# Sliding-window attention and a routed MoE: q and k by head on a partition, turned by 64-column products

## Chip, cores and metric

One core of a Trainium2 chip. The metric is the device time of one execution in microseconds (us); lower is better. The kernel before takes 766.49 us (median of three runs, 764.59 to 767.16). The profiled execution has a span of 762.4 us from its first to its last instruction; the views below count from that span's start.

## What is computed

Eight batches with eight heads each of 576 positions with head size 64 go through causal attention with a window of 64. The result, 4608 rows of 512, goes through a layer with eight experts, in which every row goes to the one expert with the highest gate value. All data are float32.

```python
scores = scale * np.matmul(q, k.transpose(0, 1, 3, 2))
rel = pos[:, None] - pos[None, :]
mask = (rel >= 0) & (rel < 64)
attn = softmax(np.where(mask, scores, -1e9))
x = np.matmul(attn, v)                  # (8, 8, 576, 64), then (4608, 512)
logits = x @ w_gate                     # 8 experts
idx, gate = argmax(logits), softmax(logits)[idx]
out = gate * (np.maximum(x @ w1[idx], 0) @ w2[idx])   # w1: 512 x 1024, w2: 1024 x 512
```

## The kernel before

The attention works on 16 units: a pair of batches (`bg`) by a pair of heads (`g`). A unit has 9 tiles of 128 query positions, and is worked off in three steps of three tiles, so 48 steps. The first 512 positions of each batch (`SM`) are loaded with four consecutive positions on one partition (`NV` = 4); the last 64 of each, the "rests", are loaded for all heads at once. The scores need q and k turned, so that the head dimension lies on the partitions: the 64 of the first head on partitions 0 to 63, those of the second on 64 to 127.

Loads of q and k for a unit, one DMA for each batch, tensor and head. On a partition, the two heads of a position lie side by side, 64 values each:

```python
def load_qk(u):
    bg, g = units[u]
    qks[u] = [qk_m(((u % 3 + 2) % 3 * 2 + n) * 1024, BG, NV, 2, D) for n in range(2)]
    for i in range(BG):
        for t, src in zip(qks[u], (q, k)):
            for h in range(2):
                nc.sync.dma_start(                                     # L487
                    out=t[:, i, :, h, :],
                    in_=src[bg * BG + i, 2 * g + h, 0:SM, :].rearrange("(p j) d -> p j d", j=NV),
                )
```

Turning them, for a step: `c` is 0 or 1 for a batch's main part, 2 for the rests. A transpose takes 128 partitions by 128 values (two heads of one position) and writes every fourth column of a PSUM bank; ScalarE copies the bank out.

```python
def turned(s):
    u, c = divmod(s, NST)
    ...
    if c == BG:
        ...                                        # rests: two full transposes, L531
        return
    for n, t in enumerate(qks[u]):
        tr = banks[next(tr_ring)](0, NV, P)
        for j in range(NV):
            nc.tensor.transpose(                                       # L539
                out=tr.rearrange("d a b -> d (a b)").rearrange("d (p j) -> d j p", j=NV)[:, j, :],
                in_=t[:, c, j].rearrange("p h d -> p (h d)"), identity=ident[:]
            )
        to = Ts[u][:, n, c * NV : (c + 1) * NV, :].rearrange("d t s -> d (t s)")
        nc.scalar.copy(out=to, in_=tr.rearrange("d a b -> d (a b)"))   # L544
```

The order in which the engines get their work is that of the program. Before the loop and in each step:

```python
load_qk(0)
nc.sync.dma_start(out=wg[:, :, 0:E], in_=...)
nc.sync.dma_start(out=x_dram[NT : NT + 1, :], in_=zrow[:])
load_rests(0)              # 4 DMAs of q and k, 2 of v, all by SyncE
load_v(0)                  # 4 DMAs of v by SyncE; 6 copies by GpSimd (L511 to L517)
load_qk(1)
load_v(1)
load_qk(2)
...
def step(s):
    if 0 <= s + 1 < N:
        prs[s + 1] = softened(*masked(s + 1, scored(s + 1)))   # L572 scores, 64x64 blocks
    if 0 <= s - 1 < N:
        px = weighted(s - 1, pTs.pop(s - 1))                   # L618, 128x64 blocks
    ripe = 0 <= s - 3 < N and logit(s - 3)                     # L655, 128x32 blocks
    if 0 <= s < N:
        pTs[s] = flipped(prs.pop(s))                           # L603, 128x128 transposes
    ...                                                        # divided(s - 1), loads of unit u + 3
    if s + 3 < N:
        turned(s + 3)                                          # L539 or L531
    if 0 <= s - 2 < N:
        x_turned(s - 2)                                        # L643, 128x128 transposes
    ...
for s in range(-3, N):
    step(s)
```

`masked` runs on VectorE (L585), `softened` on ScalarE (L595). The second half of the kernel, the experts, is left as it is.

Of the kernel before, what the change touches and what calls it, by code (L numbers as in the profile page):

```python
# [12 lines left out]
BF16 = mybir.dt.bfloat16  # L13
I32 = mybir.dt.int32
AF = mybir.ActivationFunctionType
ALU = mybir.AluOpType
# [4 lines left out]
WINDOW = 64  # L21
MASKED = -1e9
# [14 lines left out]
def kernel(  # L37
# [10 lines left out]
    nc = tc.nc  # L48
    P = nc.NUM_PARTITIONS
    B, H, S, D = q.shape  # L50
# [8 lines left out]
    NV = NB // 2  # L59
    SM = NV * P  # L60
    BG = 2
# [15 lines left out]
    consts = ctx.enter_context(tc.tile_pool(name="consts", bufs=1))  # L77
# [4 lines left out]

    ident = consts.tile([P, P], F32, name="ident")
    make_identity(nc, ident[:])
    GE = 32
    wg = consts.tile([P, NG, GE], F32, name="wg")
    nc.gpsimd.memset(wg[:], 0.0)
# [12 lines left out]
    V, G = nc.vector, nc.gpsimd  # L100
# [76 lines left out]
    with tc.tile_pool(name="tmp", bufs=1) as tmp:  # L177
# [8 lines left out]
        for i in range(BG):  # L186
            iota(tok_g[:, :, i * NV : (i + 1) * NV], pattern=[[BG * S, NJ // NTB], [P, NV]], base=i * S,
                 channel_multiplier=1)
            iota(tok_g[i * D : (i + 1) * D, :, BG * NV], pattern=[[BG * S, NJ // NTB]], base=i * S + SM,
                 channel_multiplier=1)  # L190
# [8 lines left out]
            out=before[:], in_=ones[:], pattern=[[1, P]], compare_op=ALU.is_gt, fill=0.0, base=0,  # L199
# [34 lines left out]


    VW = D + 1
    ST = 3
    NST = NTB // ST
    UT = NTB * P
    qk_m = Memory(consts.tile([P, 10240], F32, name="qk_m"))  # L240
# [199 lines left out]
    with tc.manual_schedule(), ExitStack() as held, ExitStack() as brief:  # L440
# [3 lines left out]
        att = brief.enter_context(tc.tile_pool(name="att", bufs=2))  # L444
        xp = brief.enter_context(tc.tile_pool(name="xp", bufs=3))
        sc_ring, tr_ring = cycle((0, 1)), cycle((2, 3, 4, 5))


        NM = 2 + ST
        mask = consts.tile([P, NM, P], BF16, name="mask")  # L450
        nc.gpsimd.memset(mask[:], 0.0)
        for h in range(2):
            for m0, m1, first in ((0, 1, False), (1, 2, h == 0), (2, NM, False)):
                rows = slice(h * D, (h + 1) * D)
                sel = partial(
                    nc.gpsimd.affine_select, out=mask[rows, m0:m1, :], in_=mask[rows, m0:m1, :], fill=MASKED,
                )
                if first:
                    sel(pattern=[[0, m1 - m0], [-1, P]], compare_op=ALU.is_ge, base=0, channel_multiplier=1)
                else:  # L460
                    sel(pattern=[[0, m1 - m0], [1, P]], compare_op=ALU.is_gt, base=0, channel_multiplier=-1)
                    sel(pattern=[[0, m1 - m0], [-1, P]], compare_op=ALU.is_ge, base=WINDOW, channel_multiplier=1)
        NVR = 3
        v_ring = []
        for i in range(NVR):
# [12 lines left out]

        def load_qk(u):
            bg, g = units[u]
            qks[u] = [qk_m(((u % 3 + 2) % 3 * 2 + n) * 1024, BG, NV, 2, D) for n in range(2)]
            for i in range(BG):
                for t, src in zip(qks[u], (q, k)):
                    for h in range(2):
                        nc.sync.dma_start(  # L487
                            out=t[:, i, :, h, :],
                            in_=src[bg * BG + i, 2 * g + h, 0:SM, :].rearrange("(p j) d -> p j d", j=NV),
                        )  # L490

        def load_rests(bg):

            at = 6144 + bg % 2 * 2048
            vr = qk_m(at + 1024, BG, H, D)
            rests[bg] = [qk_m(at, H, D), qk_m(at + 512, H, D), vr]
            for t, src in zip(rests[bg], (q, k)):
                for i in range(BG):
                    nc.sync.dma_start(
                        out=t[i * D : (i + 1) * D], in_=src[bg * BG + i, :, SM:S, :].rearrange("h p d -> p h d")  # L500
                    )
            for i in range(BG):
                nc.sync.dma_start(out=vr[D:P, i], in_=v[bg * BG + i, :, SM:S, :].rearrange("h p d -> p h d"))

        def load_v(u):
            bg, g = units[u]
            va, vb = v_ring[u % NVR]
            for i in range(BG):
                for h in range(2):
                    nc.sync.dma_start(out=va[:, i, :, h, 0:D], in_=whole(v, u, i, h))  # L510
                G.tensor_copy(out=vb[D:P, i, NV - 1, :, 0:D], in_=rests[bg][2][D:P, i, 2 * g : 2 * g + 2])  # L511

                nc.gpsimd.tensor_copy(  # L513
                    out=vb[0:D, i].rearrange("p j h d -> p (j h d)"),
                    in_=va[D:P, i].rearrange("p j h d -> p (j h d)"),
                )
                nc.gpsimd.tensor_copy(  # L517
                    out=vb[D:P, i, 0 : NV - 1].rearrange("p j h d -> p (j h d)"),
                    in_=va[0:D, i, 1:NV].rearrange("p j h d -> p (j h d)"),
# [6 lines that stand above are left out]
            if c == 0:  # L526
                Ts[u] = qkT_m(u % 2 * 2 * NTB * P, 2, NTB, P)
            if c == BG:
                tr = banks[next(tr_ring)](0, NV, P)
                for n, t in enumerate(rests[bg][0:2]):  # L530
                    nc.tensor.transpose(  # L531
                        out=tr[:, n, :], in_=t[:, 2 * g : 2 * g + 2].rearrange("p h d -> p (h d)"), identity=ident[:]
                    )
                nc.scalar.copy(out=Ts[u][:, :, BG * NV, :], in_=tr[:, 0:2, :])
                return
            for n, t in enumerate(qks[u]):
                tr = banks[next(tr_ring)](0, NV, P)
                for j in range(NV):
                    nc.tensor.transpose(  # L539
                        out=tr.rearrange("d a b -> d (a b)").rearrange("d (p j) -> d j p", j=NV)[:, j, :],  # L540
                        in_=t[:, c, j].rearrange("p h d -> p (h d)"), identity=ident[:]
                    )
                to = Ts[u][:, n, c * NV : (c + 1) * NV, :].rearrange("d t s -> d (t s)")
                nc.scalar.copy(out=to, in_=tr.rearrange("d a b -> d (a b)"))  # L544

# [32 lines left out]
        def masked(s, scs):  # L578

            m0 = (1, 0, 2)[s % NST]  # L580
            prs = [att.tile([P, ST, P], F32, name=f"pr{h}") for h in range(2)]
            mx = small.tile([P, 2, ST], F32, name="mx")
            for h in range(2):
                for m in range(ST):
                    V.tensor_tensor_reduce(  # L585
                        out=prs[h][:, m, :], in0=scs[h][:, m, :], in1=mask[:, m0 + m, :], scale=-scale, scalar=-2 * MASKED,
                        op0=ALU.add, op1=ALU.min, accum_out=mx[:, h, m : m + 1],
                    )
            return prs, mx

        def softened(prs, mx):
            for h in range(2):
                for m in range(ST):
                    y = prs[h][:, m, :]
                    nc.scalar.activation(out=y, in_=y, func=AF.Exp, scale=-1.0, bias=mx[:, h, m : m + 1])  # L595
            return prs
# [276 lines left out]
            gather_first(perm_e[:, 0:C])  # L873

        N = NU * NST
        load_qk(0)
        nc.sync.dma_start(out=wg[:, :, 0:E], in_=moe_w_gate.rearrange("(g p) e -> p g e", p=P))
        nc.sync.dma_start(out=x_dram[NT : NT + 1, :], in_=zrow[:])
        load_rests(0)
        load_v(0)  # L880
        load_qk(1)
        load_v(1)
        load_qk(2)

        for g in range(NG):
            step = NST * (g // 2) + g % 2 + 1
# [7 lines left out]

        prs, pTs = {}, {}
        def step(s):
            if 0 <= s + 1 < N:
                prs[s + 1] = softened(*masked(s + 1, scored(s + 1)))
            if 0 <= s - 1 < N:
                px = weighted(s - 1, pTs.pop(s - 1))  # L900
            ripe = 0 <= s - 3 < N and logit(s - 3)
            if 0 <= s < N:
                pTs[s] = flipped(prs.pop(s))
            if 0 <= s - 1 < N:
                divided(s - 1, px)
            if s >= 0 and s % NST == 0:
                u = s // NST
                if u + 3 < NU and (u + 3) % NG == 0:
                    load_rests((u + 3) // NG)
                if u + 2 < NU:  # L910
                    load_v(u + 2)
                if u + 3 < NU:
                    load_qk(u + 3)
            if s + 3 < N:
                turned(s + 3)
            if 0 <= s - 2 < N:
                x_turned(s - 2)
            for op in todo.pop(s, ()):
                op()
            if ripe:  # L920
                bg, c = (s - 3) // (NG * NST), (s - 3) % NST
                parts = by_tokens(bg, c)
                next(parts)
                todo.setdefault(s + 1, []).append(partial(next, parts, None))
                if c == NST - 1:
                    after(s + 1, choose(bg), bg)


        for n, s in enumerate((N - 6, N - 3)):
            fs = slice(n * HF, (n + 1) * HF)  # L930
            todo.setdefault(s, []).append(partial(nc.sync.dma_start, out=w2s[0][:, fs], in_=w2v[0][:, fs]))
        for s in range(-3, N):
            step(s)
        assert not todo
        sums_w2(0)
# [135 lines left out]
```

## Time and profile before

| what | value |
|---|---|
| time, median of 3 | 766.49 us |
| span of the profiled execution | 762.4 us, mean granted TensorE clock 0.986 |
| attention stage, until the last step's weighted sums | 0 to about 199 us |
| TensorE busy, 0 to 10 and 10 to 20 us | 4.46 and 5.33 us |
| TensorE busy, 40 to 60 and 100 to 120 us | 19.86 and 20.00 us |
| DMA share, 0 to 10 and 10 to 20 us | 0.57 and 1.07 |
| DMA share, 40 to 60 and 100 to 120 us | 0.87 and 0.86 |
| moved over the span | 94.55 MB in 137,620 packets, 117,072 of them under 512 B |

A line of the timeline gives the start in us, the time until the last of the merged instructions has ended, the engine, the kernel's line, the operation with its output and inputs, for TensorE the rows and columns of the stationary block (128*64: 128 rows, 64 columns), the shape and the count; in brackets, how long the engine had been idle before, and what ended that. "SPq" is SyncE's queue: its lines are issues of DMAs, not the transfers. A line of the table of waits gives who waited for whom, the total in us, how often, and the longest.

### The profile page before, as it was taken

How to read it: one execution, taken by the hardware profiler on the slowest of the kernel's cores; microseconds unless marked ns; L12 is line 12 of the kernel's file. 1: busy time of each engine (PE TensorE's matmuls, PEld its weight loads, DVE VectorE, ACT ScalarE, POOL GpSimd, SP SyncE). 2: the span in 40 equal slices, each digit the busy share in tenths (PEclk: the TensorE clock that was granted, in tenths of full speed). 3: DMA queues.
4: the chain of work that ended last, by engine and by line, in shares of the span. 5: the costliest groups of instructions: out<-in, count | busy, mean ns of one | idle time of the engine just before them, and what ended most of it. 6: DMA issues, size and time to landing. Idle time of an engine off the chain costs nothing. (4 is left out here: it accounts for less than half of the span.)

```text
span 762.4 us, 18401 instructions
## 1 busy us (share of the span) xinstructions
PE 720.1 (94%) x7018; PEld 650.5 (85%) x7018; DVE 395.0 (52%) x1355; ACT 268.4 (35%) x676; POOL 357.1 (47%) x366
## 2 busy tenths in 40 slices
PE   4999999999899999999999999999999999999995
PEld 3888888887688988998999899899988899988994
DVE  2677997988758544523542353352434452424432
ACT  4888888887543201211121122011220121211220
POOL 5215558593860635537531653663266465262111
PEclk8999999999899999999999999999999999999998
DMA  8997889983513712604410360542171171101101
GB/s 162 226 205 173 175 181 255 213 225 113 195 42 126 277 58 67 229 29 138 159 56 30 96 208 30 166 142 70 31 257 45 40 254 56 43 24 42 43 29 54
DMA packets 137620, 94.55 MB, mean 124 GB/s; under 512 B 117072, under 2 KB 117072, under 8 KB 137490
## 3 DMA queue, kind: packets, MB, share of 16 engines
q1 hardware_dynamic: 127858, 62.16, 29.8%
q0 software_dynamic: 9056, 28.58, 11.7%
q10 hardware_dynamic: 576, 2.10, 0.8%
q8 instruction: 78, 1.28, 0.7%
q14 instruction: 52, 0.43, 0.2%
HBM read 73.94 MB, written 20.45 MB: 124 GB/s over the span
## 5 line engine op out<-in xcount | busy, mean ns | idle before, releaser
L322 PE MATMUL bank<-qk_m,s 128*128 128x128 f32 x1216 | 145.4, 275 | 0.0
L322 PEld LDWEIGHTS bank<-qk_m,s 128*128 128x128 f32 x1216 | 140.4, 192 | 0.0
L322 PE MATMUL bank<-qk_m,w 128*128 128x128 f32 x912 | 112.2, 276 | 12.5 <-DVE v_m L358 8.8
L272 POOL DMA_INDIRECT qk_m<-x_dram,at_g x42 | 44.6, 1063 | 167.5 <-PE bank L303 160.2
L322 PEld LDWEIGHTS bank<-qk_m,w 128*128 128x128 f32 x912 | 106.7, 192 | 17.5 <-issue 17.3
L595 ACT ACTIVATE pr<-pr,mx 128x128 f32<-128x128 f32 x288 | 89.7, 390 | 31.8 <-DVE mx L585 31.5
L358 DVE TENSOR_TENSOR v_m<-bank,v_m 128x256 f32<-128x256 f32 x101 | 40.8, 422 | 110.1 <-PE bank L362 54.8
L585 DVE CUSTOM_DVE_ANT_0 pr<-bank,mask 128x128 f32<-128x128 f32 x288 | 64.4, 286 | 27.7 <-PE bank L572 26.1
L329 ACT COPY qk_m<-bank 128x512 f32<-128x512 f32 x19 | 11.2, 587 | 165.7 <-PE bank L322 155.2
L292 POOL DMA_INDIRECT out_dram<-v_m,at_s x42 | 42.4, 1010 | 56.5 <-DVE v_m L358 44.7
L139 POOL TENSOR_TENSOR s<-w 128x1024 f32<-128x1024 f32 x22 | 52.3, 2376 | 19.1 <-DMA qk_m<-x_dram,at_g 14.8
L362 PE MATMUL bank<-qkT_m,v_m 128*128 128x256 f32 x240 | 54.0, 380 | 1.7 <-DVE v_m L139 1.7
L362 PEld LDWEIGHTS bank<-qkT_m,v_m 128*128 128x128 f32 x240 | 45.4, 190 | 8.5 <-DVE v_m L139 2.5
L362 PE MATMUL bank<-qk_m 128*128 128x256 f32 x224 | 52.1, 380 | 0.0
L513 POOL COPY v_m<-v_m 64x520 f32<-64x520 f32 x32 | 19.8, 618 | 67.0 <-DMA v_m<-in_v_dram 59.7
L618 PEld LDWEIGHTS bank<-v_m,pT 128*64 128x64 f32 x1152 | 40.5, 139 | 11.6 <-DVE xs L632 5.8
L618 PE MATMUL bank<-v_m,pT 128*64 128x65 f32 x1152 | 47.2, 229 | 2.6 <-DVE xs L632 2.6
L362 PE MATMUL bank<-s,v_m 128*128 128x256 f32 x216 | 48.1, 379 | 0.0
L362 PEld LDWEIGHTS bank<-qk_m 128*128 128x128 f32 x224 | 41.5, 190 | 5.5 <-ACT v_m L374 0.4
L362 PEld LDWEIGHTS bank<-s,v_m 128*128 128x128 f32 x216 | 41.0, 190 | 5.6
L572 PE MATMUL bank<-qkT_m 64*64 64x128 f32 x1152 | 44.8, 286 | 0.1
L539 PE MATMUL bank<-ident,qk_m 128*128 128x128 f32 x256 | 36.6, 287 | 8.7 <-DMA qk_m<-in_q_dram 8.1
(167 smaller groups left out, 1220.7 us busy)
## 6 DMA issues: line engine op xcount, KB each, us to landing
w<-in_moe_w_dram SPq DMA_DIRECT2D x11, 2048.0 KB, 9.2
qk_m<-in_q_dram SPq DMA_DIRECT2D x72, 128.0 KB, 3.8
qk_m<-in_k_dram SPq DMA_DIRECT2D x72, 128.0 KB, 3.7
v_m<-in_v_dram SPq DMA_DIRECT2D x64, 128.0 KB, 3.7
qk_m<-in_moe_w_dram SPq DMA_DIRECT2D x3, 2048.0 KB, 16.1
x_dram<-xs POOLq DMA_DIRECT2D x6, 512.0 KB, 4.8
x_dram<-xs POOLq DMA_DIRECT2D x3, 768.0 KB, 5.3
w<-in_moe_w_dram ACTq DMA_DIRECT2D x4, 512.0 KB, 5.0
```

Of the source, the lines that this page charges most:

```text
L139: op()
L272: G.indirect_dma_start(out=xg[c], out_offset=None, in_=x_dram[:, :], in_offset=bass.IndirectOffsetOnAxis(ap=at_g[:, c : c + 1], axis=0),)
L292: put = G.indirect_dma_start(out=out[:, :], out_offset=bass.IndirectOffsetOnAxis(ap=at_s[:, c : c + 1], axis=0), in_=ys[c], in_offset=None ...
L322: nc.tensor.matmul(acc[:, f, :], lhsT=a[:, g, f * P : (f + 1) * P], rhs=b[:, g, :], start=(first and f == 0 and g == 0), stop=(g == HG - 1 ...
L358: plus = lambda out, a, b: V.tensor_tensor(out=out, in0=a, in1=b, op=ALU.add)
L362: nc.tensor.matmul(acc, lhsT=a[:, f, :], rhs=b[:, f, :], start=(start and f == 0), stop=(stop and f == HF - 1), skip_group_check=True,)
L513: nc.gpsimd.tensor_copy(out=vb[0:D, i].rearrange("p j h d -> p (j h d)"), in_=va[D:P, i].rearrange("p j h d -> p (j h d)"),)
L539: nc.tensor.transpose(out=tr.rearrange("d a b -> d (a b)").rearrange("d (p j) -> d j p", j=NV)[:, j, :], in_=t[:, c, j].rearrange("p h d - ...
L572: nc.tensor.matmul(out_, lhsT=qT[rows, t, a * WINDOW : (a + 1) * WINDOW], rhs=rhs, start=True, stop=True, skip_group_check=True,)
L585: V.tensor_tensor_reduce(out=prs[h][:, m, :], in0=scs[h][:, m, :], in1=mask[:, m0 + m, :], scale=-scale, scalar=-2 * MASKED, op0=ALU.add, ...
L595: nc.scalar.activation(out=y, in_=y, func=AF.Exp, scale=-1.0, bias=mx[:, h, m : m + 1])
L618: nc.tensor.matmul(px[a * D : (a + 1) * D, h, m, :], lhsT=pTs[h][:, m, a * D : (a + 1) * D], rhs=vt[:, h, :], start=True, stop=True, skip_ ...
```

## The change

Four things, all in the attention stage:

1. On a partition, q and k now lie by head and then by position. So the four positions of a head are 1 KB in one piece, in DRAM as in SBUF, and one DMA loads both heads of a batch.
2. The two heads of one position no longer lie side by side, so the full transpose is replaced by two matrix products with the identity, one for each head: the 128x64 block is stationary, the identity moves, and the result goes to 64 partitions of the bank.
3. The first loads are issued by three engines: q by SyncE, k by ScalarE, the rests of q and k by GpSimd. The gate weights and the zero row are loaded after the second unit's q and k. To have the masks in time, GpSimd builds them ahead of its other constants.
4. The first step's scores are computed before the second turn, where the loop had all three first turns around them.

```diff
-        def load_qk(u):
+        def load_qk(u, *engines):
             bg, g = units[u]
-            qks[u] = [qk_m(((u % 3 + 2) % 3 * 2 + n) * 1024, BG, NV, 2, D) for n in range(2)]
+            qks[u] = [qk_m(((u % 3 + 2) % 3 * 2 + n) * 1024, BG, 2, NV, D) for n in range(2)]
             for i in range(BG):
-                for t, src in zip(qks[u], (q, k)):
-                    for h in range(2):
-                        nc.sync.dma_start(
-                            out=t[:, i, :, h, :],
-                            in_=src[bg * BG + i, 2 * g + h, 0:SM, :].rearrange("(p j) d -> p j d", j=NV),
-                        )
+                for t, src, engine in zip(qks[u], (q, k), engines):
+                    engine.dma_start(
+                        out=t[:, i].rearrange("p h j d -> p h (j d)"),
+                        in_=src[bg * BG + i, 2 * g : 2 * g + 2, 0:SM, :].rearrange("h (p j) d -> p h (j d)", j=NV),
+                    )
 ...
-        def load_rests(bg):
+        def load_rests(bg, engine=nc.sync):
 ...                                        # q and k by this engine, v by SyncE as before
+                by_p = tr.rearrange("d a b -> d (a b)").rearrange("d (p j) -> d j p", j=NV)
                 for j in range(NV):
-                    nc.tensor.transpose(
-                        out=tr.rearrange("d a b -> d (a b)").rearrange("d (p j) -> d j p", j=NV)[:, j, :],
-                        in_=t[:, c, j].rearrange("p h d -> p (h d)"), identity=ident[:]
-                    )
+                    for h in range(2):
+                        nc.tensor.matmul(
+                            by_p[h * D : (h + 1) * D, j, :], lhsT=t[:, c, h, j, :], rhs=ident[:],
+                            start=True, stop=True, skip_group_check=True,
+                        )
 ...
-        load_qk(0)
+        load_qk(0, nc.sync, nc.scalar)
+        load_rests(0, G)
+        load_v(0)
+        load_qk(1, nc.sync, nc.sync)
         nc.sync.dma_start(out=wg[:, :, 0:E], in_=moe_w_gate.rearrange("(g p) e -> p g e", p=P))
         nc.sync.dma_start(out=x_dram[NT : NT + 1, :], in_=zrow[:])
-        load_rests(0)
-        load_v(0)
-        load_qk(1)
         load_v(1)
-        load_qk(2)
+        load_qk(2, nc.sync, nc.sync)
 ...
-            if 0 <= s + 1 < N:
+            if 0 < s + 1 < N:
                 prs[s + 1] = softened(*masked(s + 1, scored(s + 1)))
 ...
-        for s in range(-3, N):
+        turned(0)
+        first = masked(0, scored(0))
+        turned(1)
+        prs[0] = softened(*first)
+        for s in range(-1, N):
             step(s)
```

The block that builds the masks is moved, unchanged, from the start of the attention stage to right behind the identity. Later loads of q and k stay with SyncE.

More of the change, by code (lines that the diff above doesn't have):

```diff
@@ L84 @@
     make_identity(nc, ident[:])
+    ST = 3
+    NM = 2 + ST
+    mask = consts.tile([P, NM, P], BF16, name="mask")
+    nc.gpsimd.memset(mask[:], 0.0)
+    for h in range(2):
+        for m0, m1, first in ((0, 1, False), (1, 2, h == 0), (2, NM, False)):
+            rows = slice(h * D, (h + 1) * D)
+            sel = partial(
+                nc.gpsimd.affine_select, out=mask[rows, m0:m1, :], in_=mask[rows, m0:m1, :], fill=MASKED,
+            )
+            if first:
+                sel(pattern=[[0, m1 - m0], [-1, P]], compare_op=ALU.is_ge, base=0, channel_multiplier=1)
+            else:
+                sel(pattern=[[0, m1 - m0], [1, P]], compare_op=ALU.is_gt, base=0, channel_multiplier=-1)
+                sel(pattern=[[0, m1 - m0], [-1, P]], compare_op=ALU.is_ge, base=WINDOW, channel_multiplier=1)
     GE = 32
@@ L236 @@
     VW = D + 1
-    ST = 3
     NST = NTB // ST
@@ L446 @@
         sc_ring, tr_ring = cycle((0, 1)), cycle((2, 3, 4, 5))
-        NM = 2 + ST
-        mask = consts.tile([P, NM, P], BF16, name="mask")
-        nc.gpsimd.memset(mask[:], 0.0)
-        for h in range(2):
[L453 to L456, printed above, removed]
-                )
[L458 to L462, printed above, removed]
         NVR = 3
@@ L477 @@
         )
-        def load_qk(u):
+        def load_qk(u, *engines):
             bg, g = units[u]
-            qks[u] = [qk_m(((u % 3 + 2) % 3 * 2 + n) * 1024, BG, NV, 2, D) for n in range(2)]
+            qks[u] = [qk_m(((u % 3 + 2) % 3 * 2 + n) * 1024, BG, 2, NV, D) for n in range(2)]
             for i in range(BG):
-                for t, src in zip(qks[u], (q, k)):
-                    for h in range(2):
-                        nc.sync.dma_start(
-                            out=t[:, i, :, h, :],
-                            in_=src[bg * BG + i, 2 * g + h, 0:SM, :].rearrange("(p j) d -> p j d", j=NV),
-                        )
-        def load_rests(bg):
+                for t, src, engine in zip(qks[u], (q, k), engines):
[4 more added lines that the diff above has]
+        def load_rests(bg, engine=nc.sync):
             at = 6144 + bg % 2 * 2048
@@ L498, in load_rests @@
                 for i in range(BG):
-                    nc.sync.dma_start(
+                    engine.dma_start(
                         out=t[i * D : (i + 1) * D], in_=src[bg * BG + i, :, SM:S, :].rearrange("h p d -> p h d")
@@ L537, in turned @@
                 tr = banks[next(tr_ring)](0, NV, P)
+                by_p = tr.rearrange("d a b -> d (a b)").rearrange("d (p j) -> d j p", j=NV)
                 for j in range(NV):
-                    nc.tensor.transpose(
-                        out=tr.rearrange("d a b -> d (a b)").rearrange("d (p j) -> d j p", j=NV)[:, j, :],
-                        in_=t[:, c, j].rearrange("p h d -> p (h d)"), identity=ident[:]
-                    )
+                    for h in range(2):
+                        nc.tensor.matmul(
+                            by_p[h * D : (h + 1) * D, j, :], lhsT=t[:, c, h, j, :], rhs=ident[:],
+                            start=True, stop=True, skip_group_check=True,
+                        )
                 to = Ts[u][:, n, c * NV : (c + 1) * NV, :].rearrange("d t s -> d (t s)")
@@ L912, in step @@
                 if u + 3 < NU:
-                    load_qk(u + 3)
+                    load_qk(u + 3, nc.sync, nc.sync)
             if s + 3 < N:
```

## The prediction

> **What bounds the kernel now.** I read the page first, then the stage in which the changed lines run, then the first 25 us of it. On the page, TensorE is busy nearly everywhere, and no other engine is close to it over the whole span:
>
> ```profile
> PE 720.1 (94%) x7018; PEld 650.5 (85%) x7018; DVE 395.0 (52%) x1355; ACT 268.4 (35%) x676; POOL 357.1 (47%) x366
> ...
> PE   4999999999899999999999999999999999999995
> ...
> DMA  8997889983513712604410360542171171101101
> ```
>
> The reader is to see two things. TensorE (second line, slices of 19 us) misses work only in the first slice. The DMA engines are 70 to 90% busy in the first nine slices, the attention stage, and little afterwards. The change touches only the attention stage, 0 to about 199 us, so I ask what ends the wait there. The table of waits for TensorE, restricted to 25 to 200 us, is nearly empty:
>
> ```profile
> PE bank L618 <- DVE xs L632: 1.5, 4, 0.5
> PE bank L643 <- DVE pT L605: 1.4, 1, 1.4
> ```
>
> That is 3 us of 175, and no DMA is in it. So between 25 and 200 us the stage takes what TensorE's own instructions take, one after the other: a faster load there is worth nothing, a longer TensorE block is paid in full. How long a block takes is read from the timeline of TensorE, where the first column is the start, so the difference of two starts is the time that a block really holds the engine (the second column contains the pipeline's tail):
>
> ```profile
> 100.02 0.42 PE L655 MATMUL bank<-xT,wg 128*32 128x128 f32 x6
> 100.37 0.88 PE L603 MATMUL bank<-ident,pr 128*128 128x128 f32 x6
> 101.08 1.04 PE L539 MATMUL bank<-ident,qk_m 128*128 128x128 f32 x8
> 101.96 0.49 PE L643 MATMUL bank<-ident,xs 128*128 128x128 f32 x3
> 102.38 0.89 PE L572 MATMUL bank<-qkT_m 64*64 64x128 f32 x24
> 103.19 0.97 PE L618 MATMUL bank<-v_m,pT 128*64 128x65 f32 x24
> 104.09 0.42 PE L655 MATMUL bank<-xT,wg 128*32 128x128 f32 x6
> ```
>
> One step of the attention is 104.09 - 100.02 = 4.07 us. L539 is the line that the change rewrites: eight full transposes, 101.96 - 101.08 = 0.88 us, so 0.11 us each (the starts of single ones in the trace are 109 ns apart).
>
> The start is different. There TensorE waits for loads:
>
> ```profile
> 4.94 2.04 PE L539 MATMUL bank<-ident,qk_m 128*128 128x128 f32 x8 [4.94 <-DMA qk_m<-in_q_dram]
> ...
> 13.23 0.30 PE L531 MATMUL bank<-ident,qk_m 128*128 128x128 f32 x1 [1.55 <-DMA qk_m<-in_k_dram]
> ...
> 18.32 2.28 PE L539 MATMUL bank<-ident,qk_m 128*128 128x128 f32 x8 [2.88 <-DMA qk_m<-in_q_dram]
> 20.53 1.35 PE L572 MATMUL bank<-qkT_m 64*64 64x128 f32 x24
> ```
>
> and SyncE's queue shows why the last of them is so late:
>
> ```profile
> 0.81 1.36 SPq L487 DMA_DIRECT2D qk_m<-in_q_dram  x2
> ...
> 13.78 1.24 SPq L487 DMA_DIRECT2D qk_m<-in_q_dram  x2
> ```
>
> The loads for the second unit (two heads of two batches) are only issued at 13.78 us, since SyncE issues everything, at about 0.65 us for one load, and 20 loads stand ahead of them. From the scores that start at 20.53 us (third step) on, TensorE runs without a real break.
>
> **What the Trainium skill says.** (1) TensorEngine Tiling (Array Packing), Key Properties: tiles of the array work in parallel, and a change of the tiling mode drains the engine. The trace agrees with both. The 24 score products of L572 (64*64) come in six rounds of four, 109 ns from round to round; and wherever the shape in the rows above changes, time is lost (worked out below). (2) TensorE: Matmul & The Clock Gate, LDWEIGHTS: the load time goes with the columns. 128 columns would be 107 ns by it (an estimate from that page); the 109 ns between transposes agree, so two loads of 64 columns cost no more than one of 128. (3) DMA: Bandwidth & Descriptors, Specifications: a transfer needs at least 512 B for line rate. The trace's packet records agree: 256 B take 18.8 ns (13.6 B/ns), 2 KB take 91.6 ns (22.4 B/ns). (4) The same page, Issuing engines are not separate DMA queues: several issuers save only issue time. Issue time is what the start above is short of.
>
> **The change part by part.**
>
> *64-column products.* In 32 of the 48 steps, L539's eight transposes of 128x128 become sixteen products of a 128x64 stationary block with the 128 columns of the identity. The two heads of a pair write partitions 0-63 and 64-127, so they lie on two column tiles and can run together: eight rounds of 109 ns, as before, 0.87 us. But L603 before it and L643 behind it stay at 128*128. Where today one mode runs through (L603, L539, L643), there will be two more changes of mode. What one costs, from the starts above:
> - Into narrower tiles: L643 has three transposes, 3 x 0.109 = 0.327, but holds 0.42, so 0.09 is lost ahead of L572. In L572 the first round takes 160 ns instead of 109 (single starts in the trace), 0.05 more. Together 0.145.
> - Back to 128*128: L655 has two rounds of three, 0.218, the first 0.024 longer, but holds 0.35, so 0.108 is lost ahead of L603; and L603 has 6 x 0.109 = 0.654 but holds 0.71, so its first is 0.056 longer. Together 0.164.
> The sum is 0.31 us per step. The steps with c = 2 keep L531's full transposes and pay nothing. Of the 32 blocks, three (s = 0, 1, 3) lie in the start, where TensorE waits anyway; 29 x 0.31 = **+9.0 us**, all on the path.
>
> *Pieces of 1 KB.* The 128 main loads of q and k (128 KB in 512 pieces of 256 B) become 64 of 256 KB in 256 pieces of 1 KB. Between the two packet times above, 1 KB should take about 50 ns (an interpolation), so the DMA engines' work for them falls from 65,536 x 18.8 / 16 = 77 us to 16,384 x 50 / 16 = 51 us. After 25 us no wait of TensorE is for a DMA, so these 26 us are hidden: **0**, except in the start.
>
> *Start: issue, order, first scores.* Ahead of the second unit's q and k, SyncE now issues two loads of q, two of the rests of v and four of v: eight instead of 20. At 0.65 us each it comes to them at 0.8 + 8 x 0.65 = 6 us instead of 13.78. ScalarE issues k beside it. GpSimd issues the rests of q and k, behind its masks: those end at 7.9 us today, with some small fills behind them about 7.5 to 8; at some 0.7 us each (its stores, 8.9 us for 12) the last goes out at about 11 and lands at 12.5 to 13. The data: first unit 4 x 0.8 us (16 packets of 50 ns on each engine), ten loads of rests and v at 32 x 18.8 ns = 0.6 us, 6 us, and the first half of the second unit, 1.6 us: 10.8 us of DMA from about 1.6 us on, so it lands at about 12.5 to 14. TensorE then still has the rests' two transposes, the second scores (0.9), flips (0.8) and the second unit's first turn (1.2): the third step's scores start at about 16.2 instead of 20.5. **-4.3 us**, likely between -2.5 and -6. The first scores being moved ahead of the second turn helps VectorE and ScalarE start, but the next scores wait for the rests all the same, so I add nothing for it.
>
> *The sum:* 766.5 + 9.0 - 4.3 = 771.2; I take off 0.7 because the few waits in the stage can swallow a little of the added time: 770.5 us.
>
> **The rivals.**
> - *The start is worth more than the modes cost.* For it: 20.5 us pass before TensorE runs through, and its work until then is only some 10 us. Against it: rests, v and 256-B pieces remain, and the GpSimd queue comes late. At best the third scores start at 13.5: -7 us, which with +9.0 makes 768; if the drain is also only half of what I read, 764.
> - *The two column tiles do not run together.* Then a block takes 16 x 0.109 = 1.74 us, +0.87 a step, 29 times, so +25 beyond mine: about 795. Against it: L618, on column tiles of the same width, does 24 products of 65 columns in 0.90 us, which is 37 ns each; one by one at half of 109 ns they would take 1.3 us. And L655 starts three products 7 ns apart on three column tiles.
> - *The loads were the limit after all,* and the freed 26 us of DMA time shorten the stage. Against it: no DMA among TensorE's waits, and a period of 4.07 us that is explained by the blocks alone. I give it almost nothing.
> - *A new wait at GpSimd:* issuing four loads delays its copies of v (six of 0.3 to 0.6 us per unit), which the first weighted sums need. It would take 1 to 3 us off the start's gain: 772 to 774.
>
> **Range and chances.** Drain 6 to 10 us, start -2.5 to -7: from 766.5 + 6 - 7 = 765.5 to 766.5 + 10 - 2.5 = 774. Products that pair worse than the scores do, or another wait, widen it to 763 to 779. The bound of 2% is 15.3 us, 751 or 782: neither end is near, only the serial column tiles would pass the upper one.
>
> **What would show it.** In the timeline after, the rewritten block, shown as 128*64 in sixteens, should hold about 1.0 us from its start to that of the next block, with a gap ahead of it and behind it, and the step should grow from 4.07 to about 4.38 us, while the steps with c = 2 stay at 3.42. The third step's scores should start at 15 to 18 us instead of 20.53. DMA busy in the first nine slices should fall, with no change for TensorE there. From 200 us on nothing should change but the offset. I am wrong if the step stays at 4.07 us (the drain is not paid between these two shapes), if it grows by over 0.6 us (no pairing), or if the third scores start before 14 or after 19 us.

## The result, and the profile after

The changed kernel takes 795.34 us (median of four runs, 795.16 to 795.49) against 766.38 us for the kernel before: ratio 1.0381, 95% interval 1.0363 to 1.0399. It is 3.8% slower. The prediction was 770.5 us, with a range of 763 to 779, and is wrong.

From the page of the changed kernel, the rows that answer to those shown of before, and one of the group table (name, shapes, count, then busy time, mean of one, and idle time before):

```profile
PE 753.9 (95%) x7786; PEld 677.5 (85%) x7786; DVE 394.2 (50%) x1355; ACT 273.6 (34%) x676; POOL 360.0 (45%) x370
...
PE   4999999999989999999999999999999999999995
...
DMA  9954648555352371351521152171152161111101
...
L540 PE MATMUL bank<-ident,qk_m 128*64 128x128 f32 x1024 | 65.1, 281 | 4.4 <-DMA qk_m<-in_q_dram 4.4
```

TensorE is as full as before, and for longer. The DMA engines have become idler in the attention stage, as intended, and nothing came of it. The count in the last row is the finding: the program has 512 of these products, the profile shows 1024 matmuls. TensorE's total grew from 7018 to 7786 matmuls, by 768: 1024 came, 256 transposes went. On the page of before, the same can be read from the scores (L572) and the transposes (L539):

```profile
L572 PE MATMUL bank<-qkT_m 64*64 64x128 f32 x1152 | 44.8, 286 | 0.1
L539 PE MATMUL bank<-ident,qk_m 128*128 128x128 f32 x256 | 36.6, 287 | 8.7 <-DMA qk_m<-in_q_dram 8.1
```

One step of the attention, in TensorE's timeline of the changed kernel (first column the start; differences of starts are what counts):

```profile
102.39 0.42 PE L656 MATMUL bank<-xT,wg 128*32 128x128 f32 x6
102.74 0.88 PE L604 MATMUL bank<-ident,pr 128*128 128x128 f32 x6
103.54 1.97 PE L540 MATMUL bank<-ident,qk_m 128*64 128x128 f32 x32
105.44 0.55 PE L644 MATMUL bank<-ident,xs 128*128 128x128 f32 x3
105.92 0.89 PE L573 MATMUL bank<-qkT_m 64*64 64x128 f32 x24
...
107.63 0.42 PE L656 MATMUL bank<-xT,wg 128*32 128x128 f32 x6
```

The rewritten block holds TensorE 105.44 - 103.54 = 1.90 us instead of 0.88, its neighbours lose 0.09 (L604, 0.80 instead of 0.71) and 0.06 us (L644, 0.48 instead of 0.42): a step takes 5.24 us (107.63 - 102.39) or 5.25 instead of 4.07.

The start, same view:

```profile
14.94 0.44 PE L530 MATMUL bank<-ident,qk_m 128*128 128x128 f32 x1 [3.39 <-DMA qk_m<-in_q_dram]
17.48 0.44 PE L530 MATMUL bank<-ident,qk_m 128*128 128x128 f32 x1 [2.10 <-DMA qk_m<-in_k_dram]
17.86 1.56 PE L573 MATMUL bank<-qkT_m 64*64 64x128 f32 x24
19.35 1.54 PE L604 MATMUL bank<-ident,pr 128*128 128x128 f32 x6
20.82 2.34 PE L540 MATMUL bank<-ident,qk_m 128*64 128x128 f32 x32
23.09 0.89 PE L573 MATMUL bank<-qkT_m 64*64 64x128 f32 x24
```

The third step's scores (last row) start at 23.09 us, 2.56 us later than before, and not 4.3 us earlier. TensorE waited for the rests of q (3.39 us) and of k (2.10 us), which GpSimd had issued:

```profile
7.36 0.93 POOL L498 DMA_DIRECT2D qk_m<-in_q_dram  x1
...
9.33 1.38 POOL L498 DMA_DIRECT2D qk_m<-in_k_dram  x2
```

Where the 31.1 us of longer span (793.5 - 762.4) are: 2.6 up to the third scores; from there to the last step's scores 211.4 us instead of 183.1 (203.63 - 20.53 before, 234.50 - 23.09 after), 28.3 more; behind them 559.0 instead of 558.8. The 29 rewritten blocks in the middle part would be 29 x 1.18 = 34.2; the waits of before swallowed 5.9, such as the one that makes one step 5.7 us long in both kernels.

### The profile page after: what moved, and what is told of

Same layout as the page of the kernel before. It is cut to its first block, busy times and chain, and to the rows that moved or that the text cites. A ratio compares the mean times of both kernels' runs of the same rounds, so it can differ in the third digit from the quotient of the medians.

```text
span 793.5 us, 19832 instructions
## 1 busy us (share of the span) xinstructions
PE 753.9 (95%) x7786; PEld 677.5 (85%) x7786; DVE 394.2 (50%) x1355; ACT 273.6 (34%) x676; POOL 360.0 (45%) x370
## 2 busy tenths in 40 slices
DMA packets 85525, 94.57 MB, mean 119 GB/s; under 512 B 48464, under 2 KB 64848, under 8 KB 85394
## 5 line engine op out<-in xcount | busy, mean ns | idle before, releaser
L540 PE MATMUL bank<-ident,qk_m 128*64 128x128 f32 x1024 | 65.1, 281 | 4.4 <-DMA qk_m<-in_q_dram 4.4
L540 PEld LDWEIGHTS bank<-ident,qk_m 128*64 128x64 f32 x1024 | 57.2, 140 | 9.7 <-POOL mask L100 4.4
L545 ACT COPY qkT_m<-bank 128x512 f32<-128x512 f32 x64 | 37.2, 586 | 22.9 <-PE bank L540 22.6
```

What stands on the lines that cost most here:

```text
L540: nc.tensor.matmul(by_p[h * D : (h + 1) * D, j, :], lhsT=t[:, c, h, j, :], rhs=ident[:], start=True, stop=True, skip_group_check=True,)
```

## The experiments

The theory after the result: a float32 product with the identity runs as two matmuls, a float32 transpose as one, so the block doubled. Rivals: the column tiles do not run together (the rival in the prediction that named 795 us); the changes of mode cost more than I had read; the new layout or the start carry the loss. All ratios are to runs of the kernel before on the same chip.

### Products alone, in the kernel before

```diff
-                    nc.tensor.transpose(out=..., in_=t[:, c, j].rearrange("p h d -> p (h d)"), identity=ident[:])
+                    for h in range(2):
+                        nc.tensor.matmul(by_p[h * D : (h + 1) * D, j, :], lhsT=t[:, c, j, h, :], rhs=ident[:], ...)
```

> The kernel before, with the eight full transposes replaced by sixteen 64-column products with the identity and nothing else changed (old layout in 256 B pieces, old loads, old order). Theory 'passes': in the trace of the changed kernel the 512 products of the program are 1024 matmul records, two for each float32 product against one for a transpose, so a rewritten block holds TensorE 1.9 us instead of 0.88, and a step takes 5.25 us instead of 4.07. Then this kernel alone loses nearly the whole: 792 to 797 us. Rival 'layout': the head-major pieces, the issuers or the start carry a part of the loss; then it is below 785 us.

Measured: 793.18 us, ratio 1.0339 (1.0313 to 1.0365); the step is 5.25 us. The products carry 26.5 of the 29 us, in the old layout with the old start. "Layout" falls as the main cause; 2.4 us remain for the layout and the start together, and the layout was not run alone.

### Full products: the second pass without column tiles

The kernel before, each transpose replaced by one product of the same 128x128 block:

```diff
-                    nc.tensor.transpose(out=..., in_=..., identity=ident[:])
+                    nc.tensor.matmul(..., lhsT=t[:, c, j].rearrange("p h d -> p (h d)"), rhs=ident[:], start=True, stop=True, ...)
```

> The kernel before, with each of the 256 full transposes replaced by one product of the same 128x128 block with the identity: no column tiles, no change of mode, old layout, old start. Theory 'passes': a float32 product is two matmul records, so a block of eight is 16 x 0.109 = 1.74 us instead of 0.88, a step grows by 0.87 to 4.94 us; 29 blocks are 25 us, less some 5 us that the waits of before swallow: 785 to 790 us. Rival 'it is the column tiles or the mode changes': 766 to 770 us.

Measured: 787.0 us, ratio 1.0281 (1.0259 to 1.0303). In its timeline the same eight blocks appear as sixteen matmuls:

```profile
102.84 1.95 PE L539 MATMUL bank<-ident,qk_m 128*128 128x128 f32 x16
104.63 0.49 PE L644 MATMUL bank<-ident,xs 128*128 128x128 f32 x3
```

104.63 - 102.84 = 1.79 us, 0.112 for each of the sixteen, the pace of a transpose, but twice as many. Neither tiles nor mode changes are in this kernel. The step is 4.98 us. So the second pass by itself is worth 0.91 us a step and 21 us.

### One pass, everything else as changed

The changed kernel with one-pass operands; it leaves out the lower 16 bits of q and k.

```diff
-                            ... lhsT=t[:, c, h, j, :], rhs=ident[:],
+                            ... lhsT=t[:, c, h, j, :].bitcast(BF16)[:, 1::2], rhs=ident_b[:],
```

> The changed kernel, its products fed with the upper 16 bits of q and k read as bf16 and a bf16 identity: the lower 16 bits of q and k are left out. Layout, column tiles, mode changes and number of products in the program stay. Theory 'passes': 512 records instead of 1024; a block falls from 1.9 us to at most 1.2 us (8 rounds of 0.109 and 0.31 for the two mode changes), a step to 4.5 us or less, the time to 778 us or less. Rival 'column tiles or mode changes are what costs': the block stays near 1.9 us and the time above 790 us.

Measured: 771.51 us, ratio 1.0066 (1.0041 to 1.0091).

```profile
104.40 0.87 PE L606 MATMUL bank<-ident,pr 128*128 128x128 f32 x6
105.21 1.06 PE L542 MATMUL bank<-ident_b,qk_m 128*64 128x128 bf16 x16
106.20 0.55 PE L646 MATMUL bank<-ident,xs 128*128 128x128 f32 x3
106.68 0.89 PE L575 MATMUL bank<-qkT_m 64*64 64x128 f32 x24
```

Sixteen matmuls, in pairs 0.109 us apart, 0.99 us for the block, 4.34 us for the step. This step is the one that I had predicted: 0.27 us above the old one where I had 0.31. That the time fits as well, 771.5 us where I had 770.5, is luck: the third scores come at 22.38 us, 1.9 later than before where I had counted 4.3 earlier, but from there to the last step's scores (209.80 us) only 4.3 of the 29 x 0.27 = 7.8 us arrive. The waits of before swallow 3.5, where I had taken off 0.7.

### Pairs of column tiles taken apart

```diff
-                for j in range(NV):
-                    for h in range(2):
+                for h in range(2):
+                    for j in range(NV):
```

> The changed kernel with the loop over heads outside that over positions, so that eight products in a row go to the same column tile. Theory 'two passes, in pairs': pairs with the other column tile are lost, 32 passes of 0.109 us one after the other, the block grows from 1.9 to about 3.6 us, 29 blocks add some 50 us: about 845 us. Rival 'no pairing, the sixteen products run one by one already' (the rival of the prediction that named 795 us): nothing is there to be lost, the time stays at 795 us.

Measured in a single run: 812.66 us, 17 us more than the changed kernel.

```profile
100.91 2.57 PE L540 MATMUL bank<-ident,qk_m 128*64 128x128 f32 x32
103.41 0.55 PE L644 MATMUL bank<-ident,xs 128*128 128x128 f32 x3
```

The block is 2.50 us instead of 1.90. "No pairing" falls, since there was something to lose. My 845 us was too much, and my text said eight products in a row where the edit puts four, that is eight matmuls, since q and k are worked off one after the other. In the middle of the block single matmuls mostly start 51 to 58 ns apart, at its ends 109 ns. So a part of the two heads' products still overlaps, although they now lie eight matmuls apart; how the engine arranges that, these records don't show.

### The start alone

The kernel before with the changed start (masks, issuers, order, first scores), old layout and full transposes.

> The kernel before with the start of the changed one (masks earlier, k by ScalarE, rests of q and k by GpSimd, second unit's loads earlier, first scores moved up), but the old layout and the full transposes. Theory 'late rests': the rests issued by GpSimd land at 15 to 17.5 us behind what SyncE has queued, later than the 11 to 13 us of before, so the third step's scores start at 22 to 24 us instead of 20.5 and the time is 767 to 770 us. Rival 'the start was good and only the long products in it made it late': third scores before 20 us, 762 to 766 us.

Measured: 766.6 us, ratio 0.9997 (0.998 to 1.0014): no difference, and in neither of the two ranges. The rests are nearly as late as in the changed kernel, the third scores 1.0 us later than before (22 to 24 us expected):

```profile
13.99 0.45 PE L531 MATMUL bank<-ident,qk_m 128*128 128x128 f32 x1 [1.78 <-DMA qk_m<-in_q_dram]
16.48 0.45 PE L531 MATMUL bank<-ident,qk_m 128*128 128x128 f32 x1 [2.04 <-DMA qk_m<-in_k_dram]
...
21.52 0.89 PE L572 MATMUL bank<-qkT_m 64*64 64x128 f32 x24
```

### Another issuer for the rests

```diff
-        load_rests(0, G)
+        load_rests(0, nc.scalar)        # or nc.sync
```

> The kernel before with the changed start, old layout and full transposes, but the rests of q and k issued by ScalarE behind its loads of k instead of by GpSimd. Theory 'GpSimd's late rests took the start's gain': they land by about 10 to 12 us, the third step's scores start at 16 to 19 us instead of 21.5, and the time is 761 to 765 us. Rival 'the DMA engines are full in the first 20 us whoever issues': third scores at 20 to 22 us, 765 to 768 us.

> As the run with ScalarE's rests, but the rests of q and k are issued by SyncE, ahead of v and of the second unit. Theory 'GpSimd's late rests': rests by 9 to 11 us, but the second unit's q and k go out some 3 us later than with ScalarE, so the third scores start at 18 to 20 us: 763 to 766 us. Rival 'DMA engines full': 765 to 768 us.

> The run with ScalarE's rests, with the turn of the rests moved behind the second unit's first turn, so that the second step's scores no longer wait for the rests. If TensorE's order in the start is what costs, the second scores start at about 12 us instead of behind the rests and the third at 15 to 18 us: 760 to 764 us, 1 to 2 us better than without the move. If the second unit's loads are what ends the wait, no difference to that run.

Measured: ScalarE 764.55 us, 0.9985 (0.9971 to 0.9998); SyncE 763.97 us, 0.998 (0.9968 to 0.9991); ScalarE with the later turn 764.49 us, 0.9988 (0.9978 to 0.9999). The times of the three can't be told apart. In the third scores, the order between ScalarE (18.69 us) and SyncE (17.72) came out the other way round than expected: with ScalarE, its first copy had to stand behind eight issues, and TensorE waited 3.4 us for it. With SyncE the rests no longer hold anything up:

```profile
11.60 0.38 PE L531 MATMUL bank<-ident,qk_m 128*128 128x128 f32 x2
...
17.72 0.89 PE L572 MATMUL bank<-qkT_m 64*64 64x128 f32 x24
```

The third scores start at 17.72 us, 2.8 earlier than before, which shows that the late rests had eaten the start's gain. That GpSimd issued them is not what made them slow: in the run of the start alone, GpSimd's four loads, issued from 7.3 to 9.9 us, took 5.2 to 6.4 us from issue to landing, and loads of q and k that SyncE issued from 8.9 to 11.0 us took 5.5 to 6.6. In the kernel before, SyncE's rests, issued from 7.4 to 9.4 us, took 2.8 to 3.7. Between 3 and 18 us the DMA share was 1.24 in the run of the start alone and 0.92 before. So the rests were issued late, into full DMA engines, behind loads that were not needed yet; issued earlier, by SyncE from 3.8 us on, they were there in time. The rival is right that the engines are full, and wrong that it makes no difference.

But only 1.8 us of the gain reach the end (765.79 - 763.97), because most of the head start, 3.1 us by then, is lost at one place, where 0.8 us remain:

```profile
51.66 0.63 PE L539 MATMUL bank<-ident,qk_m 128*128 128x128 f32 x4 [1.01 <-DMA qk_m<-in_q_dram]
53.20 0.63 PE L539 MATMUL bank<-ident,qk_m 128*128 128x128 f32 x4 [0.91 <-DMA qk_m<-in_k_dram]
```

SyncE had issued these loads from 47.88 us on; in the kernel before it issued them from 47.95 us on. TensorE was 3 us ahead, the loads were not.

Moving the turn of the rests behind the second unit's turn added nothing that can be told apart: the third scores then waited for the rests' copy.

### Moving the weights out of the head start's way

```diff
-            step = NST * (g // 2) + g % 2 + 1       # loads of the first expert's w1: steps 1, 2, 4, 5
+            step = NST * (g + 2)                    # 6, 9, 12, 15; third run: 5 + 2 * g
-            todo.setdefault(3 * NST + n, []).append(op)   # their sums, GpSimd: steps 9 to 12
+            todo.setdefault(7 * NST + n, []).append(op)   # 21 to 24; third run: 14 + n
```

> The run with the rests issued by SyncE, with the four loads of the first expert's weights moved from steps 1, 2, 4 and 5 to steps 6, 9, 12 and 15, and the four sums on them from steps 9 to 12 to steps 21 to 24. In that run 3.1 us of head start shrank to 0.8 us in one step, at 51.7 and 53.2 us, where TensorE waited for loads of q and k. Theory 'the head start runs into the weights on the DMA engines': those two waits go, 2 us or more of the head start last to the end, 761 to 763 us. Rival 'the loads of q and k in 256 B pieces are themselves too slow for a head start': the wait comes all the same or later, 763 to 765 us.

> The kernel before with only the first expert's weights and their sums moved to later steps, as in the run beside it. After 25 us its TensorE has no wait for a DMA, so both theories expect no change: 765 to 766.5 us. If it is faster by over 1.5 us, the weights cost the kernel before something that its waits do not show.

> The run with the rests issued by SyncE, with the first expert's weights loaded in steps 5, 7, 9 and 11 and their sums in steps 14 to 17, so ahead of the gate products and stores that GpSimd does from about step 20 on and with which the sums collided when they stood in steps 21 to 24 (VectorE then waited 10.4 us for stores). Theory 'the head start runs into the weights': with the collision gone, no wait for q and k at 51 to 53 us, 761 to 763.5 us. Rival 'the head start cannot last, since the loads of q and k are about as slow as the stage': 763.5 to 766 us.

Measured: 772.33 us, 1.0076 (1.0059 to 1.0094); alone in the kernel before 774.44 us, 1.0109 (1.009 to 1.0129); third run 771.25 us, 1.0053 (1.0031 to 1.0075). Three misses, all for a cause that I had not looked at: neither of the two other places that I gave the sums on GpSimd is free. In the first (its profile is of the slowest of six runs, 777.23 us), the table of waits of VectorE has

```profile
DVE xs L632 <- DMA x_dram<-xs: 10.4, 2, 5.9
```

10.4 us for stores that GpSimd issued late, since the sums stood ahead of them. In the third the sums meet VectorE's routing instructions. The timelines of GpSimd and of VectorE there:

```profile
98.89 2.35 POOL L919 TENSOR_TENSOR s<-w 128x1024 f32<-128x1024 f32 x1
101.20 2.34 POOL L919 TENSOR_TENSOR s<-w,s 128x1024 f32<-128x1024 f32 x1
```

```profile
99.38 1.89 DVE L739 TENSOR_SCALAR r_half<-r_pos 128x9 int32<-128x9 int32 x1
101.31 2.26 DVE L740 CAST rkhi<-r_half 128x9 f32<-128x9 int32 x1
103.60 0.17 DVE L741 TENSOR_SCALAR r_half<-r_pos 128x9 int32<-128x9 int32 x1
```

An instruction on 128x9 values takes 1.89 or 2.26 us while a sum of GpSimd runs, and 0.17 behind it; the next scores' masking waits for VectorE all that while. Whether the weights are what the head start runs into was not answered: in the first of these runs there was no wait at 51 us, but also no head start left (its fourth scores at 24.67 us, as before), and in the third the wait came, at 52 to 55 us, some 6 us behind a load of weights.

The lowest median of all versions is that of the start with SyncE's rests, old layout and full transposes: 0.2% below the kernel before.

## Why the prediction was wrong, point by point

- **What bounds the kernel:** right. TensorE's own instructions set the stage's time, and of the added 34.2 us 28.3 were paid. The 0.7 us that I let the waits swallow was too little, it was 5.9. One slip: the stage does not end at 199 us, as I wrote and as the table above has it; the last step's scores start at 203.63 us.
- **64-column products, "eight rounds of 109 ns, as before, 0.87 us":** this is the step that failed. It counted 16 products as 16 matmuls. There are 32, in 16 rounds of two: 16 x 0.109 = 1.74 us. The page of before had said so twice, in the two rows shown with the result: 48 steps with 12 score products each are 576, and L572 is there with 1152 matmuls; L539 has 256 for 256 transposes. I read the pace of one matmul off the timeline and not the counts, and took the 24 matmuls of a step's scores for 24 products. Nor does the pace follow the columns of the stationary block, as I had it: 64-column matmuls alone at the ends of the block with the heads apart start 109 ns apart too.

  The Trainium skill has the fact on a page that I had not drawn on: FP8 and Floating Point Precision, TensorE Precision Notes, says that true float32 takes four passes through the array. What the traces show of it is two matmul records for each product, each at the pace of a transpose; how four passes would lie in two records, no run here shows. The second record was worth 0.91 us a step and 21.2 us of the 29.0 (full products).
- **Two changes of mode, 0.31 us a step, +9.0:** right. 0.27 us in two comparisons: 4.34 against 4.07 us (one pass), and 5.25 against 4.98 us (column tiles against full products). Over the whole run that is 29 x 0.27 = 7.8 us; between the two kernels with products it is 5.3 us in the medians (793.2 - 766.6 less 787.0 - 765.8) and 8.3 us in the profiled spans (791.0 - 782.7; that of the full products is of the fastest of its four runs).
- **The rival "column tiles do not run together, about 795":** the number is that of the result, and the mechanism is not. Its reading (0.109 us for each of sixteen) gives the same 1.74 us as two passes in pairs, and so its sign, a step longer by over 0.6 us, came true for another cause. The two matmuls of a pair start 6 or 7 ns apart in the trace, and taking them apart cost another 17 us.
- **Pieces of 1 KB, 0:** right as far as shown. 1 KB took 53 ns in the mean (I had 50), the packets fell from 137,620 to 85,525, and in the rest of the attention stage after 25 us TensorE waits for no DMA in either kernel. Over the span the DMA engines worked some 17 us less, not 26: 39.4% of 793.5 us by the page's queues, against 43.2% of 762.4 us.
- **Start, -4.3:** wrong in sign, +2.6. SyncE came to the second unit's loads at 6.44 us (I had 6), and GpSimd issued the rests between 7.36 and 10.7 us (I had 11). But they landed by 14.9 and 17.5 us, where I had 12.5 to 13. I had given the last of them 1.5 to 2 us from its issue at 11 us to its landing. From issue to landing SyncE's rests took 2.8 to 3.7 us in the kernel before; here GpSimd's took 5.6 to 7.3 us, and SyncE's loads of v beside them, issued from 9.6 to 10.7 us, 6.3 to 7.2. I had counted the queue at the DMA engines for the second unit's loads, and not for the rests. And behind the wait TensorE ran at half clock: the granted clock was 0.50 from 17 to 21 us, so the scores there took 1.49 us instead of 0.81 and the flips 1.47 instead of 0.80. My sum used the blocks' warm times.

## What to carry to other kernels

Count the matmuls of a group in the profile against the products that the program writes before using its mean time: in these traces a float32 product ran as two matmuls and a float32 transpose as one, so a product with the identity is no like-for-like stand-in. Where one engine is full, price a change on that engine first: here some 17 us less DMA work ended no wait of TensorE. And a gain at the start lasts only as far as the next place where another resource was just keeping up, here at 51 to 53 us; check who waits later before counting it to the end.

## What the runs showed of the hardware that I had not expected

- A float32 128x128 product held TensorE 0.22 us (1.79 us for eight), a transpose of the same block 0.11 us.
- Four loads of 128 KB issued by GpSimd between 7.4 and 10.7 us, beside a busy SyncE queue, had landed only by 17.5 us; issued by SyncE from 3.8 us on, none held up TensorE at 11.6 us. SyncE's loads that were issued at the same time as GpSimd's took as long to land, which points to the full DMA engines (DMA share 1.22 between 3 and 18 us) and not to the issuer.
- Two VectorE instructions that take 0.17 us otherwise took 1.9 and 2.3 us beside GpSimd's float32 sums. The Trainium skill, SBUF — State Buffer, Who interferes with whom, says that the two engines share a pair of ports as a lock, which casts and tensor_scalar can take too; this trace, with one of each, agrees.
